# Attention and hard-swish MLP on one core: a planner that counts three modes of TensorE, finer constants, keys chosen anew

## The chip, the cores and the metric

The kernel runs on one core of a Trainium2 chip. The metric is the device time of one execution in microseconds (us). Three runs of the kernel before gave 583.2, 583.35 and 584.42 us; the median is 583.35 us.

## The reference

Causal attention over 4 batches and 12 heads (448 positions, head size 64), whose output becomes the 1792 x 768 input of a two-layer MLP with a hard-swish between the layers, all in float32.

```python
scores = scale * np.matmul(q, k.transpose(0, 1, 3, 2))
scores = np.where(mask, -1000000000.0, scores)       # causal
attn = np.exp(scores - max); attn = attn / (attn.sum + 1e-09)
x = (attn @ v) as 1792 x 768
h = x @ w_in                                          # 768 x 2048
g = h * np.clip(h + 3.0, 0.0, 6.0) / 6.0
out = g @ w_out                                       # 2048 x 768
```

## The kernel before, in words

The attention is cut into 24 units: a unit is one batch and one pair of heads. The MLP is cut by batch: batches 0 and 1 are computed alone (`first_layer`, `early_products`, `middle`), batches 2 and 3 together at the end with a Strassen-like scheme (`last_x`, `last_first`, `last_second`).

A unit is this chain. Scores: 8 row blocks (two heads e, four blocks i of 112 queries), in two operations, blocks 3 and 2 together and blocks 1 and 0 together (`products`, line 490). The two heads stand in the upper and the lower 64 rows of the array, so their matmuls run beside each other. Units 0 to 5 take float32 operands in one pass; the others split them in a high and a low part and take three matmuls each. Then VectorE adds the mask and takes the row minimum (line 505), ScalarE takes the exponential and its sum (line 512), VectorE the reciprocals (lines 522 and 523), and GpSimd, ScalarE or VectorE scale the rows (lines 533 and 531). TensorE turns the 20 blocks of 112 x 112 in six groups (line 553), ScalarE or VectorE copy each group from its PSUM bank (lines 361 and 364), and TensorE multiplies by v (line 566); there the two heads stand in two halves of 64 columns. The result is split into two parts again and is one of the MLP's operands.

Every product of the MLP is three matmuls of a 128 x 128 weight tile with 448 columns, on lines 640, 641 and 642. So TensorE's instructions are of three shapes: the whole array (lines 640 to 642, and the turns on line 553), two halves of rows (scores, line 490), two halves of columns (line 566).

The weights are made once from two 32-bit words each on VectorE (`words`, lines 603, 605 and 608), kept in DRAM and loaded again for later batches. ScalarE rounds them to a high part (line 361), VectorE or GpSimd subtract it for the low part (line 373).

The order of all this is not written by hand. `Flow` is a planner that runs while the program is built. Every operation has a key, made from a table of due times (`T_...`, `UNIT`, `LOADS`, `WORDS`, `K_...`), an expected duration, the engines that may take it, and what it reads and writes. At each step an engine takes the ready operation with the lowest key for which there is a buffer. Several engines may take the copies and the scalings; a lag says how much later one of them may. TensorE has one rule more: if the operation is of another mode than the last, the planner looks further for one of the same mode with a key at most `KEEP[mode]` later, and if it takes the other, it adds `SWITCH / 2` to the time. Before, there are two modes: `tiled` is true for scores and for the product with v, and false for all else, so going from one of these two to the other costs the planner nothing. Between 20 and 36 us of its own time the planner also writes in matmuls without use (`fill`, line 1072) where it expects TensorE to wait. At the start, `WARM` matmuls on a constant run before the first loads have landed (line 1092).

Of the kernel before, what the change touches and what calls it, by code (L numbers as in the profile page):

```python
# [19 lines left out]
C = 112  # L20
# [10 lines left out]

T_FIRST = -113
T_PACE = 4
T_EARLY = 8
T_EACH = 11
T_LATE = 74
T_DENSE = 7.25
T_LOAD = -8
T_W = 10
T_WLOAD = 9  # L40
T_XA = 166
T_X = 175
T_LAST = 182
T_PAIR = 10.5
T_SECOND = T_LAST + 8 * T_PAIR
T_SECOND_GROUP = 72
T_MID = 120
T_BACK = 40
T_WORDS = 77
M_LOAD = 20  # L50
E_WORDS = 6.5
K_SCORES = 0
K_TURN = 6.5
K_TURNS = 0.6
K_PRODUCT = 14
K_GATE = 5
KEEP_FULL = 0
KEEP_TILED = 6.5
N_RAW = 6
DEPTH = 3  # L60
A_FIRST = 4
D_FIRST = 0.4
T_V = 11
FINE = 3
W_FROM = 3
W_BEHIND = 4
UNIT = [-80, -17, 5, 2.5, 0.5, -1, -2, -1.5, 5.5, 0.5, -6.5, -3, -3.5, -8, -2.5, -4.5, -1, -1.5, -6, -4.5, -2.5, 1, -4, 3]
LOADS = [-70, -38, -8, 10, 0, -10, 12, -14, -22, -4, -20, -14, 10, 4, -12, 2, -8, -12, -2, -28, -10, -4, 4, -6]
K_KEEP = -4
K_G = 4  # L70
GATE_FROM = 1
WORDS = [1, 8, -6, 4, -3, 7, -5, 0, -4, 3, -6, 0, 6, -2, 7, -4, 2, 4, 2, 3, -2, 2, -8, -4, 8, 3, -7, 5]
T_ISSUE = 0.36
NORM_LAG = 1.5
A_LAG = 0

# [7 lines left out]
    qk="d qk", op="d op", wf="d wf", sf="d sf", x="d x", pt="d pt", pr3="d pr3", pr20="d pr20", xq="d xq", xc="d xc", gt="d gt", gm="d gm", so="d so",  # L84
    ps="b s most ps", tp="b s most", av="b s", mo="b mo", c="b c",
)
MOST = dict(qk=3, op=4, wf=4, sf=6, x=8, pt=6, pr3=4, pr20=5, xq=6, xc=21, gt=12, gm=9, so=3, s=8, most=8, ps=8, mo=2, c=8)

# [22 lines left out]
class Flow:  # L111
# [5 lines left out]
    BEGIN, LATENCY = 0.8, 0.12  # L117
    SWITCH = 0.4
    TAIL = dict(PE=.1, D=.085, A=.105, P=.04, SP=0)

    KEEP = KEEP_FULL, KEEP_TILED
    QUEUE, WARM = 8, 4
    DMA_PACKET, DMA_RATE, DMA_LANES, DMA_LATENCY = 0.008, 23e3, 16, 2.1
# [8 lines left out]

    def op(self, key, ways, parts, r=(), tiled=False, nbytes=0):

        w = [x for _, _, ws in parts for x in ws]
        bufs = {x[0] for x in list(r) + w if isinstance(x[0], Buf)}
        o = Op((key, len(self.ops)), ways, parts, bufs, nbytes)
        o.tiled = tiled
        for b in bufs:
            b.refs += 1  # L140
        before = {}
        for x in list(r) + w:
            if x in self.wrote:
                a, i = self.wrote[x]
                before[a] = max(before.get(a, 0), i)
        for x in w:
            for a in self.readers.pop(x, ()):
                before[a] = len(a.parts) - 1
        for x in r:
            self.readers.setdefault(x, []).append(o)  # L150
        for i, (_, _, ws) in enumerate(parts):
            for x in ws:
                self.wrote[x] = o, i
        before.pop(o, None)
        for a, i in before.items():
            a.then.append((o, i))
        o.waits = len(before)
        self.ops.append(o)
        return o

    def run(self):
# [3 lines left out]
        busy = dict.fromkeys(lists, self.BEGIN)  # L165
        self.dma, self.mode, self.port, tick = 0.0, False, 0.0, 0
        left = len(self.ops)
# [17 lines left out]
        while events:  # L185
            now = events[0][0]
            while events and events[0][0] <= now + 1e-9:
                _, _, what, x = heappop(events)
# [17 lines left out]
            for e, cand in lists.items():  # L206
# [4 lines left out]
                for _, o in cand:  # L211
# [9 lines left out]
                    for b in o.bufs:  # L221
                        if not b.held and b.kind in ORDERED:
                            x = turns[ORDERED[b.kind]]
# [41 lines left out]
    def start(self, o, e, now, need, out, busy, post):  # L265
# [5 lines left out]
        if e == "PE" and o.tiled != self.mode:  # L271
            t += self.SWITCH / 2
            self.mode = o.tiled
# [9 lines left out]
        if e == "SP":  # L283
            self.landed.append(o.ends[-1])
            t = max([t, *self.landed[-self.QUEUE:-self.QUEUE + 1]])
# [16 lines left out]
def tile_causal_attention_hardswish_moe(ctx: ExitStack, tc: tile.TileContext, q, k, v, w_in, w_out, out):  # L302
    nc = tc.nc
# [25 lines left out]
    def ap(b):  # L329
        if b.tile is None:  # L330
            b.tile = pools[b.tag].tile(b.shape, b.dt, tag=f"{b.tag}{b.slot}", name=b.tag, bufs=1)
        return b.tile
# [11 lines left out]

    def pe(key, parts, r, tiled=False):
        flow.op(key, {"PE": (1, 0)}, [(d, lambda e, g=g: g(), w) for d, g, w in parts], r, tiled)
# [35 lines left out]
    warm = const.tile([64, C], F32, tag="warm", name="warm")  # L382
# [37 lines left out]
    def unit(b, p):  # L420
        at = NPAIR * b + p
        raw32 = at < N_RAW
# [68 lines left out]

        cost, more = (1.667e-3, .06) if raw32 else (1.25e-3, .08)
        for a, two in enumerate(((1, 0), (3, 2)) if at == 0 else ((3, 2), (1, 0))):
# [3 lines left out]
                [(cost * C * (i + 1) + more, lambda i=i: products(i), [(ps[e, i][0], i) for e in range(2)] + [("turn",)]) for i in two],  # L497
                (halves_[0] if at == a == 0 else reads) + [("unit", at - (2 if b else DEPTH))], True,
            )
# [42 lines left out]
        for e in range(2):  # L542
            for js, ph in zip(GROUPS, pairs):
# [10 lines left out]

                pe(key, [(.096 * len(blocks) + .03, turn, [(tp, 0)])], [pk[e, i] for i in sorted({i for i, _ in blocks})])
                move(
# [13 lines left out]

        pe(t + K_PRODUCT, [(10 * C * 1.667e-3, times_v, [(av, 0), (av, 1), ("unit", at)])], deps, True)
        if b < 2:
# [518 lines left out]
    for _ in range(Flow.WARM):  # L1091
        nc.tensor.matmul(ap(b)[:C, :C], warm, warm, start=True, stop=True)

# [48 lines left out]
```

## Time and profile before

| | |
|---|---|
| runs, us | 583.2, 583.35, 584.42 |
| profiled execution, us | 583.93 |
| its span, first to last instruction, us | 582.2 |
| PE busy, us | 573.8 |
| DVE, ACT, POOL busy, us | 486.7, 405.7, 233.4 |
| TensorE matmul records | 3496 |

The span is 1.73 us shorter than the profiled execution; that much lies around it. The profiled execution is 0.58 us longer than the median of the runs. A matmul's busy time in the trace is longer than the distance to the next one's start, since matmuls overlap in the array: to see what a matmul costs, one subtracts the start of one row from the start of a later one. Consecutive instructions of one group are merged into one row, with their number behind an x. A float32 matmul that is not rounded stands in the trace as two records.

### The profile page before, as it was taken

Reading aid. Unit: us, or ns where it says so; the run is one execution under the profiler, and the core shown is the slowest. Engines: PE = TensorE matmul, PEld = TensorE weight load, DVE = VectorE, ACT = ScalarE, POOL = GpSimd, SP = SyncE. Lnnn points to the kernel's source line nnn. Section 1 sums busy time; section 2 is a strip of 40 time slices with the busy share of each in tenths; the row PEclk is TensorE's granted clock in tenths of the full one; section 3 lists DMA queues with packets and bytes.
Section 4 is the critical chain, followed back from the end, with each engine's and each line's share of the span. In section 5 each row is a group of like instructions: output and inputs, shape, how many; then the busy total and the mean of one; then the engine's idle time right before and its main releaser. Section 6 shows DMA issues by size and latency. Waiting matters only on the chain.

```text
span 582.2 us, 10686 instructions
## 1 busy us (share of the span) xinstructions
PE 573.8 (99%) x3496; PEld 502.5 (86%) x3496; DVE 486.7 (84%) x1093; ACT 405.7 (70%) x973; POOL 233.4 (40%) x226
## 2 busy tenths in 40 slices
PE   8999999999999999999999999999999999999997
PEld 5667988988888788888988989899999999999996
DVE  5899999899689787999998668999888799985652
ACT  6997885888757666899988968576555586454530
POOL 2678889874447344776274212034000042100000
PEclk9999999999999999999999999999999999999999
DMA  8958999967579898999832254441211424443411
GB/s 235 334 184 278 315 319 362 395 230 233 179 267 303 258 385 267 329 381 304 301 114 76 94 165 145 160 128 56 82 55 55 128 64 135 133 133 111 138 64 48
DMA packets 61352, 115.59 MB, mean 199 GB/s; under 512 B 6512, under 2 KB 36592, under 8 KB 61296
## 3 DMA queue, kind: packets, MB, share of 16 engines
q1 hardware_dynamic: 60576, 114.34, 59.5%
q10 hardware_dynamic: 720, 0.57, 0.3%
q8 instruction: 27, 0.44, 0.3%
q14 instruction: 29, 0.24, 0.1%
HBM read 83.39 MB, written 31.49 MB: 197 GB/s over the span
## 4 chain that ended last, share of the span: by engine, by line
PE 88%; DMA 5%; DVE 3%; ACT 2%; issue 1%; SPq 0%; DVEq 0%; ACTq 0%
PE b L640 24%; PE b L641 23%; PE b L642 23%; PE b L566 7%; PE b L553 6%; PE b L490 5%; DMA gl<-in_v_dram 2%; DMA wd<-in_w_in_dram 1%; DMA wd<-in_w_out_dram 1%; ACT d L512 1%; DVE b L603 1%; DVE d L608 1%; DVE b L505 1%; DVE b L605 1%; ACT gl L512 0%
## 5 line engine op out<-in xcount | busy, mean ns | idle before, releaser
L640 PE MATMUL b<-d,wh 128*128 128x448 f32 x624 | 231.4, 371 | 0.7 <-ACT d L512 0.7
L641 PE MATMUL b<-d,wh 128*128 128x448 f32 x624 | 226.3, 363 | 0.0
L642 PE MATMUL b<-d,wl 128*128 128x448 f32 x624 | 225.7, 362 | 0.0
L640 PEld LDWEIGHTS b<-d,wh 128*128 128x128 f32 x624 | 117.2, 188 | 10.6 <-ACT d L512 1.2
L642 PEld LDWEIGHTS b<-d,wl 128*128 128x128 f32 x624 | 116.9, 187 | 9.0 <-POOL wl L373 0.4
L641 PEld LDWEIGHTS b<-d,wh 128*128 128x128 f32 x624 | 117.2, 188 | 6.3
L361 ACT CAST wh<-wd 128x768 fp32r<-128x768 f32 x88 | 73.6, 836 | 70.1 <-PE b L641 61.5
L373 DVE TENSOR_TENSOR wl<-wd,wh 128x768 fp32r<-128x768 f32 x74 | 79.7, 1077 | 26.0 <-ACT wh L361 25.0
L505 DVE CUSTOM_DVE_ANT_0 b<-b,mask 112x224 f32<-112x224 f32 (+1 forms) x192 | 80.2, 479 | 19.6 <-PE b L490 17.2
L512 ACT ACTIVATE d<-b,prow 112x448 f32<-112x448 f32 (+2 forms) x144 | 72.2, 517 | 15.5 <-DVE prow L505 13.1
L373 POOL TENSOR_TENSOR d<-d 128x896 fp32r<-128x896 f32 (+3 forms) x28 | 43.2, 1548 | 36.3 <-DVE d L373 23.4
L553 PE MATMUL b<-ident,d 112*112 112x112 f32 x384 | 55.9, 261 | 1.2 <-ACT d L512 0.8
L373 POOL TENSOR_TENSOR wl<-d,wh 128x768 fp32r<-128x768 f32 (+1 forms) x28 | 46.1, 1649 | 23.9 <-ACT wh L361 14.9
L361 ACT COPY d<-b 112x336 f32<-112x336 f32 (+1 forms) x104 | 43.7, 494 | 7.5 <-PE b L553 6.9
L553 PEld LDWEIGHTS b<-ident,d 112*112 112x112 f32 x384 | 42.7, 133 | 5.6 <-POOL gl L533 1.0
L533 POOL TENSOR_SCALAR d<-d,prow 112x112 f32<-112x112 f32 (+2 forms) x59 | 29.4, 509 | 31.7 <-DVE prow L523 25.4
L566 PE MATMUL b<-d,vr 112*64 112x224 f32 (+3 forms) x288 | 37.5, 405 | 0.0
L531 ACT ACTIVATE d<-d,prow 112x336 f32<-112x336 f32 (+2 forms) x66 | 33.8, 548 | 4.2 <-DVE prow L523 4.2
L603 DVE TENSOR_SCALAR b<-wd 128x384 int32<-128x384 int32 (+1 forms) x56 | 32.9, 613 | 3.0 <-DMA wd<-in_w_out_dram 2.5
L490 PE MATMUL b<-d 64*112 64x448 f32 (+3 forms) x432 | 35.0, 305 | 0.0
L490 PEld LDWEIGHTS b<-d 64*112 64x112 f32 x432 | 30.2, 172 | 5.5 <-issue 1.2
L566 PEld LDWEIGHTS b<-d,vr 112*64 112x64 f32 x288 | 19.1, 136 | 18.4 <-issue 10.7
(111 smaller groups left out, 934.3 us busy)
## 6 DMA issues: line engine op xcount, KB each, us to landing
wd<-in_w_in_dram SPq DMA_DIRECT2D x32, 384.0 KB, 6.0
wd<-in_w_out_dram SPq DMA_DIRECT2D x24, 512.0 KB, 6.6
wd<-kept_w SPq DMA_DIRECT2D x32, 384.0 KB, 4.7
wd<-kept_s SPq DMA_DIRECT2D x32, 384.0 KB, 3.0
kept_w<-d SPq DMA_DIRECT2D x16, 384.0 KB, 6.2
kept_w<-d SPq DMA_DIRECT2D x24, 256.0 KB, 5.4
kept_s<-d SPq DMA_DIRECT2D x24, 256.0 KB, 3.8
wd<-kept_w SPq DMA_DIRECT2D x48, 128.0 KB, 2.2
```

The costliest lines, as they stand in the source:

```text
L361: nc.scalar.copy(o(), i()) if scale is None else nc.scalar.mul(o(), i(), scale)
L373: (nc.gpsimd if e == "P" else nc.vector).tensor_tensor(o(), a(), b(), op)
L490: nc.tensor.matmul(score(e, i), qx[m, c], kx[m, :w], start=n == 0, stop=n == len(terms) - 1)
L505: lambda _, e=e, i=i, w=w: nc.vector.tensor_tensor_reduce(score(e, i), score(e, i), mask[:, S - w:], -0.125, 3.0e38, ALU.add, ALU.min, ap( ...
L512: lambda _, e=e, i=i: nc.scalar.activation(row_of(pr, e, i), score(e, i), ACTF.Exp, bias=ap(st)[:, e, i:i + 1], scale=-1.0, accum_out=ap(s ...
L531: nc.scalar.mul(x, x, ap(st)[:, e, 4 + i:5 + i])
L553: nc.tensor.transpose(ap(tp)[:C, C * n:C * n + C], row_of(pr, e, i)[:, C * j:C * j + C], ident)
L566: nc.tensor.matmul(ap(av)[64 * e:64 * e + 64, S - w:S], va()[:, j, e, :], ap(ph)[:, e, o:o + w], start=(j == 0), stop=(j == NC_ - 1),)
L603: nc.vector.tensor_scalar(ti, high, 3, 0x3FFFFFFF, ALU.logical_shift_left, ALU.bitwise_and)
L640: nc.tensor.matmul(ps, ap(wh)[:, a], xh, start=start, stop=False, skip_group_check=more)
L641: nc.tensor.matmul(ps, ap(wh)[:, a], xl, start=False, stop=False, skip_group_check=more)
L642: nc.tensor.matmul(ps, ap(wl)[:, a], xh, start=False, stop=stop, skip_group_check=more)
```

## The change

The planner's modes become three: 0 for the whole array, 1 for scores, 2 for the product with v. A change between any two costs 0.1 us of planned time, where a change between tiled and not tiled cost 0.2 us before. `KEEP` has an entry for each mode: from the whole array another mode may be left aside for an operation due at most 0.5 later (0 before), in either of the other two for 6 (6.5 before). The expected time of a score block goes from 0.08 to 0.09 us beside its columns, that of a product with v gets 0.07 us more, and that of a group of turns 0.03 us less. At the start 11 matmuls of 56 columns take the place of 4 of 112. Due times, keys, lags and numbers of buffers are new throughout.

```diff
-T_FIRST = -113
-T_PACE = 4
+T_FIRST = -94
+T_PACE = 6.5
...
-T_LOAD = -8
+T_LOAD = -20
-T_WLOAD = 9
+T_WLOAD = 14
...
-M_LOAD = 20
+M_LOAD = 11
...
-KEEP_FULL = 0
-KEEP_TILED = 6.5
+KEEP_FULL = 0.5
+KEEP_TILED = 6
...
-A_FIRST = 4
-D_FIRST = 0.4
+A_FIRST = 3.2
+D_FIRST = 0
...
-UNIT = [-80, -17, 5, 2.5, ...]
+UNIT = [-72, -19, 5, 4.5, ...]
...
-MOST = dict(qk=3, op=4, wf=4, sf=6, x=8, pt=6, pr3=4, pr20=5, xq=6, xc=21, gt=12, gm=9, so=3, s=8, most=8, ps=8, mo=2, c=8)
+MOST = dict(qk=3, op=4, wf=3, sf=8, x=8, pt=9, pr3=5, pr20=5, xq=6, xc=21, gt=12, gm=8, so=3, s=8, most=8, ps=8, mo=4, c=8)
...
-    SWITCH = 0.4
+    SWITCH = 0.1
...
-    KEEP = KEEP_FULL, KEEP_TILED
-    QUEUE, WARM = 8, 4
+    KEEP = KEEP_FULL, KEEP_TILED, KEEP_TILED
+    QUEUE, WARM = 8, 11
...
-            t += self.SWITCH / 2
+            t += self.SWITCH
...
-        cost, more = (1.667e-3, .06) if raw32 else (1.25e-3, .08)
+        cost, more = (1.667e-3, .06) if raw32 else (1.25e-3, .09)
...
-                (halves_[0] if at == a == 0 else reads) + [("unit", at - (2 if b else DEPTH))], True,
+                (halves_[0] if at == a == 0 else reads) + [("unit", at - (2 if b else DEPTH))], 1,
...
-                pe(key, [(.096 * len(blocks) + .03, turn, [(tp, 0)])], [pk[e, i] for i in sorted({i for i, _ in blocks})])
+                pe(key, [(.096 * len(blocks), turn, [(tp, 0)])], [pk[e, i] for i in sorted({i for i, _ in blocks})])
...
-        pe(t + K_PRODUCT, [(10 * C * 1.667e-3, times_v, [(av, 0), (av, 1), ("unit", at)])], deps, True)
+        pe(t + K_PRODUCT, [(10 * C * 1.667e-3 + .07, times_v, [(av, 0), (av, 1), ("unit", at)])], deps, 2)
...
-        nc.tensor.matmul(ap(b)[:C, :C], warm, warm, start=True, stop=True)
+        nc.tensor.matmul(ap(b)[:C, :C // 2], warm, warm[:, :C // 2], start=True, stop=True)
```

What this does to the order is seen at three places.

TensorE, among the first units, behind the turns of unit 1 (L553): L1072 are the matmuls without use, L490 the scores of unit 3. A minus is a row of before alone.

```order
 L553 MATMUL b<-ident,gl 112x112
 L553 MATMUL b<-ident,d 112x112 x5
-L1072 MATMUL b<-identr 112x112 x4
 L490 MATMUL b<-gh 112x448 x2
 L490 MATMUL b<-gh 112x336 x2
```

The four matmuls without use are gone here, and likewise the four at a second place, behind the turns of unit 2.

TensorE, in the first layer of batch 0, around one product with v (L566) and one unit's scores (L490), before:

```order
L642 MATMUL b<-d,wl 128x448
L566 MATMUL b<-d,vr 64x448 x2
L566 MATMUL b<-d,vr 64x336 x2
L566 MATMUL b<-d,vr 64x224 x2
L566 MATMUL b<-d,vr 64x112 x2
L490 MATMUL b<-d 112x448 x6
L490 MATMUL b<-d 112x336 x6
L490 MATMUL b<-d 112x224 x6
L490 MATMUL b<-d 112x112 x6
L640 MATMUL b<-d,wh 128x448
```

The same place now:

```order
L566 MATMUL b<-d,vr 64x448 x2
L566 MATMUL b<-d,vr 64x336 x2
L566 MATMUL b<-d,vr 64x224 x2
L566 MATMUL b<-d,vr 64x112 x2
L640 MATMUL b<-d,wh 128x448
L641 MATMUL b<-d,wh 128x448
L642 MATMUL b<-d,wl 128x448
L490 MATMUL b<-d 112x448 x6
L490 MATMUL b<-d 112x336 x6
L490 MATMUL b<-d 112x224 x6
L490 MATMUL b<-d 112x112 x6
L640 MATMUL b<-d,wh 128x448
```

Products of the MLP now stand between the product with v and the scores, so TensorE goes through three shapes with one change more. Counted over the whole program, without the matmuls without use, the changes between the three shapes go from 69 to 83; 15 of them lay among the first six units and 16 do now. The trips from the MLP's products to turns, which have the same shape, go from 51 to 31 (3 and 4 of them among the first six units). Counted as the planner did before, whole array against any half, the changes go from 47 to 75.

ScalarE, around the exponentials of unit 3 (L512), before; L361 are copies of turned blocks (112 rows) and of the products with v (128 rows):

```order
L361 COPY d<-b 112x448
L361 COPY d<-b 112x336 x2
L512 ACTIVATE d,prow<-b,prow 112x448 x2
L512 ACTIVATE d,prow<-b,prow 112x336
L361 CAST d<-b 128x448
L361 COPY r<-b 128x448
L512 ACTIVATE d,prow<-b,prow 112x336
L361 COPY d<-b 112x448
L361 COPY d<-b 112x336 x2
L361 COPY d<-b 112x448
L512 ACTIVATE gl,prow<-b,prow 112x224 x2
```

The same place now:

```order
L361 CAST d<-b 128x448
L361 COPY r<-b 128x448
L512 ACTIVATE d,prow<-b,prow 112x448 x2
L512 ACTIVATE d,prow<-b,prow 112x336 x2
L512 ACTIVATE gl,prow<-b,prow 112x224 x2
L512 ACTIVATE d,prow<-b,prow 112x112 x2
L512 ACTIVATE d,prow<-b,prow 112x448 x2
L512 ACTIVATE d,prow<-b,prow 112x336 x2
L512 ACTIVATE gl,prow<-b,prow 112x224 x2
L512 ACTIVATE d,prow<-b,prow 112x112 x2
```

The copies of unit 2's turned blocks have left ScalarE's queue here; they stand on VectorE's now. Ahead of the last exponential of unit 5 there were 14 copies of turned blocks on ScalarE and are 7.

## Rows read from the trace of the kernel before

**Rows 1.** The page's first part: busy us, share of the span, instructions.
```profile
span 582.2 us, 10686 instructions
PE 573.8 (99%) x3496; PEld 502.5 (86%) x3496; DVE 486.7 (84%) x1093; ACT 405.7 (70%) x973; POOL 233.4 (40%) x226
```

**Rows 2.** Waits of PE from 60 us to the end: us, times, longest.
```profile
PE b L640 <- ACT d L512: 0.7, 1, 0.7
```

**Rows 3.** Timeline of PE near 100 us: start, us, instruction.
```profile
98.40 0.37 PE L642 MATMUL b<-d,wl 128*128 128x448 f32 x1
98.70 2.11 PE L566 MATMUL b<-d,vr 112*64 112x448 f32 x16
100.74 1.89 PE L490 MATMUL b<-d 64*112 64x448 f32 x24
...
102.87 0.37 PE L641 MATMUL b<-d,wh 128*128 128x448 f32 x1
103.07 0.37 PE L642 MATMUL b<-d,wl 128*128 128x448 f32 x1
```

**Rows 4.** Timeline of PE around scores alone, near 212 us.
```profile
211.02 0.36 PE L642 MATMUL b<-d,wl 128*128 128x448 f32 x1
...
213.66 0.37 PE L642 MATMUL b<-d,wl 128*128 128x448 f32 x1
```

**Rows 5.** Timeline of PE around a product with v alone, near 365 us.
```profile
363.83 0.37 PE L642 MATMUL b<-d,wl 128*128 128x448 f32 x1
...
366.68 0.36 PE L642 MATMUL b<-d,wl 128*128 128x448 f32 x1
```

**Rows 6.** Timeline of PE around ten turned blocks, near 120 us.
```profile
119.32 0.37 PE L642 MATMUL b<-d,wl 128*128 128x448 f32 x1
...
119.63 0.74 PE L553 MATMUL b<-ident,d 112*112 112x112 f32 x6
120.20 0.26 PE L553 MATMUL b<-ident,pr 112*112 112x112 f32 x1
...
120.91 0.37 PE L642 MATMUL b<-d,wl 128*128 128x448 f32 x1
```

**Rows 7.** Timeline of PE among the first units.
```profile
21.98 0.60 PE L1072 MATMUL b<-identr 112*112 112x112 f32 x4
22.64 1.57 PE L490 MATMUL b<-gh 64*112 64x448 f32 x8
...
47.69 3.99 PE L566 MATMUL b<-d,gl 112*64 112x448 f32 x32 [0.17 <-DVE d L608]
```

**Rows 8.** Busy us of each engine (instructions) from 16 to 52 us, granted clock, DMA.
```profile
16.00:52.00 36.00, 35.25 (x281) 24.29 (x283) 33.06 (x112) 32.19 (x102) 27.15 (x43) 1.00 0.77 254
```

**Rows 9.** Groups by line: busy us, mean ns of one, idle before.
```profile
L361 ACT COPY d<-b 112x336 f32<-112x336 f32 (+1 forms) x104 | 43.7, 494 | 7.5 <-PE b L553 6.9
```

**Rows 10.** Timeline of DVE, three of its waits.
```profile
10.27 0.63 DVE L505 CUSTOM_DVE_ANT_0 b<-b,mask 112x448 f32<-112x448 f32 x1 [1.34 <-PE b L490]
...
21.10 0.17 DVE L522 TENSOR_SCALAR b<-prow 112x8 f32<-112x8 f32 x1 [1.60 <-ACT d L512]
...
209.65 0.69 DVE L603 TENSOR_SCALAR b<-wd 128x512 int32<-128x512 int32 x1 [1.74 <-DMA wd<-in_w_out_dram]
```

**Rows 11.** Timeline of POOL before unit 3's scalings.
```profile
32.56 1.84 POOL L373 TENSOR_TENSOR wl<-d,wh 128x768 fp32r<-128x768 f32 x1 [3.71 <-ACT wh L361]
```

**Rows 12.** Groups of POOL with 896 elements: busy, mean ns.
```profile
L368 POOL TENSOR_SCALAR d<-d 128x896 fp32r<-128x896 f32 x9 | 9.3, 1030 | 14.3 <-issue 6.3 <-PE b L490 6.2 <-DVE d L533 1.8
```

**Rows 13.** Timeline of PE at the start.
```profile
1.08 1.83 PE L1092 MATMUL b<-warm 64*112 64x112 f32 x8 [1.08 <-DVE warm L385]
...
3.58 4.08 PE L490 MATMUL b<-gh 64*112 64x224 f32 x16 [0.67 <-DMA gh<-in_k_dram]
```

**Rows 14.** Scores (line 490) of unit 1 and of unit 2: PE, PEld busy, clock, DMA.
```profile
8.42:12.15 3.73, 3.73 (x16) 2.41 (x18) 1.00 1.07 294
12.21:14.12 1.91, 1.91 (x19) 1.33 (x17) 1.00 1.06 253
```

More of the change, by code (lines that the diff above doesn't have):

```diff
@@ L37 @@
 T_DENSE = 7.25
-T_LOAD = -8
+T_LOAD = -20
 T_W = 10
-T_WLOAD = 9
-T_XA = 166
-T_X = 175
-T_LAST = 182
+T_WLOAD = 14
+T_XA = 165
+T_X = 172
+T_LAST = 180
 T_PAIR = 10.5
-T_SECOND = T_LAST + 8 * T_PAIR
+T_SECOND = 266
 T_SECOND_GROUP = 72
@@ L49 @@
 T_WORDS = 77
-M_LOAD = 20
+M_LOAD = 11
 E_WORDS = 6.5
 K_SCORES = 0
[L53 to L56, printed above, removed]
-KEEP_FULL = 0
-KEEP_TILED = 6.5
+K_TURN = 7
+K_TURNS = 0.5
+K_PRODUCT = 13
+K_GATE = 4
+KEEP_FULL = 0.5
+KEEP_TILED = 6
 N_RAW = 6
 DEPTH = 3
-A_FIRST = 4
-D_FIRST = 0.4
-T_V = 11
+A_FIRST = 3.2
+D_FIRST = 0
+T_V = 6
 FINE = 3
@@ L66 @@
 W_BEHIND = 4
[L67 to L70, printed above, removed]
+UNIT = [-72, -19, 5, 4.5, 0, -3.5, -8, 1, 4, 3.5, -6, -4, -4.5, -7.5, -8, -2.5, 1, -4.5, -2.5, -8, -6, 0.5, -5, 3]
+LOADS = [-58, -36, -8, 6, 4, -18, 2, -16, -28, -20, 12, 2, -2, -6, -6, -30, -28, -28, -14, 10, -2, -4, 8, -4]
+K_KEEP = -6
+K_G = 5
 GATE_FROM = 1
-WORDS = [1, 8, -6, 4, -3, 7, -5, 0, -4, 3, -6, 0, 6, -2, 7, -4, 2, 4, 2, 3, -2, 2, -8, -4, 8, 3, -7, 5]
+WORDS = [-2, -4, -6, -1, 3, 2, -8, -1, 6, -5, 2, 5, 5, 8, 5, -5, 3, 0, -5, 4, -3, -5, 5, -3, 5, 3, 8, 3]
 T_ISSUE = 0.36
-NORM_LAG = 1.5
-A_LAG = 0
+NORM_LAG = 0.5
+A_LAG = 0.8
 BUFS = dict(
@@ L131, in __init__, with op @@
         self.ops, self.wrote, self.readers, self.landed = [], {}, {}, []
-    def op(self, key, ways, parts, r=(), tiled=False, nbytes=0):
+    def op(self, key, ways, parts, r=(), tiled=0, nbytes=0):
         w = [x for _, _, ws in parts for x in ws]
         bufs = {x[0] for x in list(r) + w if isinstance(x[0], Buf)}
-        o = Op((key, len(self.ops)), ways, parts, bufs, nbytes)
+        o = Op((round(key, 5), len(self.ops)), ways, parts, bufs, nbytes)
         o.tiled = tiled
@@ L165, in run @@
         busy = dict.fromkeys(lists, self.BEGIN)
-        self.dma, self.mode, self.port, tick = 0.0, False, 0.0, 0
+        self.dma, self.mode, self.port, tick = 0.0, 0, 0.0, 0
         left = len(self.ops)
@@ L343, in one, with pe @@
             o.port = set()
-    def pe(key, parts, r, tiled=False):
+    def pe(key, parts, r, tiled=0):
         flow.op(key, {"PE": (1, 0)}, [(d, lambda e, g=g: g(), w) for d, g, w in parts], r, tiled)
```

## The prediction

> **What bounds the kernel now.** I read the page's first part, then PE's waits, then the timeline of PE, and at last what the other engines do where PE waits. PE is busy for 573.8 of 582.2 us and no other engine for more than 486.7 [rows 1]. That share alone proves little, since a matmul's busy time overlaps the next one's; so the waits were read. From 60 us to the end PE waits once, 0.7 us, for a bank that ScalarE frees [rows 2]. Among the first units, from 16 to 52 us, it is busy for 35.25 of 36.00 us, and there DVE (33.06) and ACT (32.19) are nearly full as well [rows 8]. So the time is made of three things: the start up to the first scores, the matmuls themselves, and what TensorE loses when it changes its shape. The matmuls of the reference are the same before and after (2088 of the MLP, 480 of scores, 192 with v, 480 turns). What is left to differ is the changes of shape, the waits, and the start.
>
> **Changes of shape.** What does one cost? Three pieces of the timeline answer it together. Each runs from one MLP matmul to the third one after the strange work, so each holds three MLP distances of 0.20 us (102.87 to 103.07). A product with v and a unit's scores in one trip: 98.40 to 103.07, 4.67 us [rows 3]. Scores alone: 211.02 to 213.66, 2.64 us [rows 4]. A product alone: 363.83 to 366.68, 2.85 us [rows 5]. The two alone make 5.49 us, the two together 4.67; the difference of 0.82 holds three MLP distances, 0.60, and the rest, 0.22 us, is the one change more that two trips have (four against three). The second place shown of the order is just this split. Each of the four starts is rounded to 0.01 us and the places differ a little, so I allow 0.18 to 0.26.
>
> The order has 14 changes more, 13 of them after the first six units: 13 x 0.22 = 2.9 us. Against this there are fewer trips to turns. One with ten turned blocks takes 119.32 to 120.91, 1.59 us, less three MLP distances 0.99 us; six turns take 119.63 to 120.20, 0.57 us, so ten take 0.95, and the trip costs 0.04 us [rows 6]. After the first units there are 48 such trips before and 27 now: 21 x 0.04 = 0.8 us go. Sum: +2.1 us, all on the path that sets the end, because PE waits nowhere there. Bounds 1.5 to 2.6 us.
>
> The Trainium skill, page "TensorEngine Tiling (Array Packing)", section Tiling Modes, says that a change of tiling mode, though not of the tile, drains the engine. By that rule rows against columns is a change like any other, and the count is 14; the 0.22 us agree. If only leaving and entering the whole array cost anything, as the planner held before, the split place would have two changes more and not one, the count would be 28 (75 - 47), and at half the price each, 0.11 us, it would come to 3.1 us in place of 2.9, which makes 583.9 us of the forecast below.
>
> **The first six units.** Two groups of matmuls without use go. One of them stands from 21.98 to 22.64 us, 0.66 us [rows 7]; the second repeats it, together 1.3 us. The scores behind each come after turns, a change of 0.2 us that stays, so 0.9 us at most come free, if the scores' operands and banks are ready then. The plain waits in this stretch are 36.00 - 35.25 = 0.75 us [rows 8]. Both together, 1.7 us, are what this stretch can give back by the rows.
>
> Will it? These waits are for the engines behind the scores. The scores' chain goes through ScalarE's exponentials, and DVE's longest wait in this stretch, 1.60 us at 21.10, is for them [rows 10]. Ahead of unit 5's last exponential ScalarE now has 7 copies fewer, and 3 scalings more, priced like a copy: 4 x 0.49 = 2.0 us less in its queue [rows 9]. The copies land on VectorE, which has fewer steps of the weights' making ahead (6 in place of 12 before unit 3's scores are done), so its queue is about as long as before. GpSimd gets the split of unit 6 ahead of unit 3's scalings; a cast of 896 elements is 1.03 us and the subtraction behind it more [rows 12], but GpSimd stood idle for 3.71 us there [rows 11]. That idle time is the cover, and if unit 6's loads are late, the cover is gone and unit 3's scalings wait behind it in GpSimd's queue, and the turns behind them. I take the whole 1.7 us, since PE had next to nothing else to wait for, and for the other end +0.6 us, a shift of a wait with nothing given back and one of about the size of the second filler put in its place. The product with v of unit 4 starts at 47.69, held by VectorE [rows 7]; it is the place where the gain has to be seen.
>
> **The start.** The 11 narrow matmuls have 11 x 56 = 616 columns in place of 4 x 112 = 448. The old ones take 1.83 us from 1.08 [rows 13]; by columns the new ones take 2.5 us and end at 3.6 us, just when the first loads have landed, at 3.58. So they cost nothing to 0.1 us, hidden by the loads; if the loads came earlier, they would be in the way by what is left of them. TensorE runs its first scores at the lower of its levels (1.2 GHz): unit 1's 16 records take 3.73 us, unit 2's 1.91, and the step lies at 12.15 us; the column of the granted clock reads 1.00 in both stretches, so the step is read from the pace [rows 14]. I take no change here. Bounds: an earlier step gives back at most DVE's wait for unit 1's scores, 1.34 us [rows 10], and nothing is lost.
>
> **Later waits and loads.** PE's 0.7 us [rows 2] comes from weights that VectorE makes late: VectorE waits 1.74 us for words from DRAM [rows 10], and the scores' masks, the exponential and the bank stand behind. These late words are held by a step of the MLP, which the change leaves, so the larger T_WLOAD doesn't bring them forward; I leave the 0.7 us in. The shorter lead of the loads in `middle` (M_LOAD 20, now 11) costs nothing while its cover holds, the other operations of TensorE between issue and use. Bounds for all later waits: -0.7 us, and +1.0, a bit more than one new wait like the present one.
>
> **Sum.** 583.93 (the profiled execution) + 2.1 - 1.7 + 0 + 0 = 584.33 us. It was 0.58 us above the median of its runs, so 583.75 against 583.35: I say 583.7 us. About 0.2%, 1.2 us, is what a measurement can tell here, so this is no change, with 582.2 and 584.5 as its limits.
>
> **Rivals.** *The waits of the first units only move* (slower). Mechanism: VectorE holds the product of unit 4 at 47.69 by its own queue, which does not get shorter, so PE comes there earlier and waits there longer. For it: DVE is busy 33.06 of 36.00 us, more than ACT. Against it: 1.60 us of what it waited was for ScalarE. Time: 583.35 + 2.1 = 585.4 us. It decides as soon as that product starts at 47.5 us or later. Chance 0.24.
>
> *All that can be freed is freed* (faster): the first units give 1.7 us, the late wait's 0.7 goes too, and the changes cost 0.18, which makes 1.5: 583.35 + 1.5 - 1.7 - 0.7 = 582.4; with the start's clock on top, at half its 1.34 us, 581.8 us. For it: the late wait hangs on one order of VectorE's queue, and all orders are new. Against it: it needs three things at once, though gaps that the modelled ends hide in the first units would help. Chance 0.24, mostly below 582.2.
>
> *The clock alone*: the longer stretch of early matmuls brings TensorE's step to 2.4 GHz forward, ahead of unit 1's scores, while the rest is as forecast: 583.7 less half of 1.34 is 583.0 us. For it: the gap between the early matmuls and the first scores, 0.67 us [rows 13], closes. Against it: the gap before unit 1's scores stays, since they wait for loads. Chance 0.10. The Trainium skill, page "TensorE: Matmul & The Clock Gate", Part 1, holds the lower clock to be the default that sustained activity releases; this rival goes by that rule, and the one step in the trace neither bears it out nor speaks against it.
>
> My forecast has the remaining 0.42.
>
> **How the numbers follow.** Faster by over 0.2%: 0.21 of the rival that frees all, 0.05 of the forecast's own spread, 0.03 of the clock: 0.29. Slower: 0.22 of the rival of moved waits, and 0.07 of the forecast, where a new later wait comes in: 0.29. Same: 0.42. The forecast's own range is 582.2 to 584.9. The range from 581.5 to 585.6 takes in both outer rivals and leaves out at the top new waits beyond one, at the bottom a clock that gives all of 1.34 us.
>
> **What would show it.** Right: a split trip of product and scores costs 0.2 us more than the joint one also in the new trace; no matmul of line 1072 left; the product of unit 4 starts near 46 us; one or two waits of PE after 60 us, together under 1.5 us. Wrong: the product of unit 4 at 47.5 us or later, waits of PE in `middle`, a step of the clock ahead of unit 1's scores, or a change of shape that costs 0.1 us as the planner says.

## The result, and the profile after

The changed kernel takes 588.29 us (median of 4 runs, 587.87 to 589.04), the kernel before, on the same chip, 583.28 us (4 runs, 582.43 to 584.42): a ratio of 1.0082, with an interval of 1.0063 to 1.0102. So it is 5.0 us slower, where 583.7 was forecast, and outside the range. The profiled execution took 589.04 us, 5.11 more than that of before.

The first part of the page after, in the columns of [rows 1]:

```profile
span 587.3 us, 10737 instructions
PE 577.9 (98%) x3502; PEld 504.5 (86%) x3502; DVE 490.6 (84%) x1101; ACT 395.5 (67%) x939; POOL 260.8 (44%) x252
```

PE is busy 4.1 us longer, and the span grew by 5.1: there is more to do and more to wait for. The waits of PE from 60 us to the end, where [rows 2] had one of 0.7 us:

```profile
PE b L640 <- DVE d L608: 1.4, 1, 1.4
PE b L553 <- DVE pr L533: 0.5, 1, 0.5
```

The timeline of PE around a place where a product with v and a unit's scores are now two trips, answering to [rows 3 to 5]:

```profile
102.19 0.37 PE L642 MATMUL b<-d,wl 128*128 128x448 f32 x1
102.48 2.11 PE L566 MATMUL b<-d,vr 112*64 112x448 f32 x16
104.52 0.47 PE L640 MATMUL b<-d,wh 128*128 128x448 f32 x1
...
105.03 0.36 PE L642 MATMUL b<-d,wl 128*128 128x448 f32 x1
...
105.63 0.36 PE L642 MATMUL b<-d,wl 128*128 128x448 f32 x1
105.92 1.90 PE L490 MATMUL b<-d 64*112 64x448 f32 x24
107.75 0.48 PE L640 MATMUL b<-d,wh 128*128 128x448 f32 x1
...
108.27 0.36 PE L642 MATMUL b<-d,wl 128*128 128x448 f32 x1
```

Each trip is read as in the prediction, from one MLP matmul to the third one behind. The product costs 105.03 - 102.19 = 2.84 us, the scores 108.27 - 105.63 = 2.64 us; together 5.48, less 0.60 for three more MLP distances, against 4.67 in one trip [rows 3]: 0.21 us for the change more.

The same rows say what the step from the product to the scores costs. The product takes 2.04 us from its first start to the next one, whether scores come next (98.70 to 100.74) or the MLP (102.48 to 104.52). The scores take 1.82 us behind the product (from 100.74 to the row below, of before) and 1.83 behind the MLP (105.92 to 107.75). So this step is not free: it costs what leaving the product for the MLP and entering the scores from the MLP cost together.

```profile
102.56 0.47 PE L640 MATMUL b<-d,wh 128*128 128x448 f32 x1
```

The start, PE's timeline, answering to [rows 13], with the first turn and the product of unit 4:

```profile
1.08 4.17 PE L1092 MATMUL b<-warm 64*112 64x56 f32 x21 [1.08 <-DVE warm L385]
4.87 0.71 PE L490 MATMUL b<-gh 64*112 64x224 f32 x1
...
5.23 9.88 PE L490 MATMUL b<-gh 64*112 64x224 f32 x47
15.75 0.28 PE L553 MATMUL b<-ident,d 112*112 112x112 f32 x1 [0.63 <-ACT d L512]
...
49.50 3.99 PE L566 MATMUL b<-d,gl 112*64 112x448 f32 x32
```

The 11 early matmuls are 22 records, 21 in the first row and the last between the first two of the scores, until 5.23 us: one every 0.19 us, as in [rows 13] (1.83 us for 8), though each has half the columns. The first scores come 1.3 us later than in [rows 13], and PE waits for no load at all: the operands were there. Where does this reach? VectorE's masks show it, answering to [rows 10]; the first row is the first mask of before, the second the same mask after, the third the sums of unit 0 after:

```profile
5.20 0.40 DVE L505 CUSTOM_DVE_ANT_0 b<-b,mask 112x224 f32<-112x224 f32 x1 [3.44 <-PE b L490]
```

```profile
6.81 0.40 DVE L505 CUSTOM_DVE_ANT_0 b<-b,mask 112x224 f32<-112x224 f32 x1 [5.04 <-PE b L490]
...
12.00 0.17 DVE L522 TENSOR_SCALAR b<-prow 112x8 f32<-112x8 f32 x1 [0.30 <-ACT d L512]
```

The wait of 1.34 us for unit 1's scores [rows 10] is gone: TensorE's records keep the pace of 2.4 GHz from 7.6 us on, ahead of these scores, where the step lay at 12.15 before [rows 14]. So VectorE runs through from 7.87 on but for 0.30 us at 12.00. All of the 1.34 us that the prediction set as a bound came back, but the first mask comes 1.6 us later than before, which is more.

PE's waits from 0 to 60 us (us in total, times, longest), and the stretch from 16 to 52 us, answering to [rows 8]:

```profile
PE b L553 <- ACT d L512: 0.9, 2, 0.6
PE b L553 <- DVE d L364: 0.4, 2, 0.2
PE b L490 <- ACT d L512: 0.4, 1, 0.4
PE b L553 <- ACT d L361: 0.3, 1, 0.3
```

```profile
16.00:52.00 36.00, 34.36 (x264) 23.38 (x264) 33.39 (x115) 30.77 (x98) 27.06 (x43) 1.00 0.66 226
```

Last, the chain of waits of the changed kernel near 180 us: start, us, what.

```profile
171.74 4.23 DMA kept_w<-d
...
178.74 7.09 DMA d<-kept_w
...
187.98 0.70 DVE d L608
188.72 0.47 PE b L640
```

Between 165 and 190 us the chain of before consists of PE's instructions alone. Here it goes through two transfers: a part of the weights goes to DRAM, comes back 7.09 us after its issue, and VectorE then makes the next words in three steps of 0.7 us, for which PE waits at 188.72.

Where the 4.89 us between the two last matmuls' ends went, summed over the distances between the starts of all matmul records: the product of unit 5 ends at 53.42 in place of 51.62 us, 1.80 later, but by then three MLP matmuls (0.6) more are done and one change (0.2) less, so 1.4 is lost. Behind that the changes of shape cost 13.03 us (67 of them) in place of 10.16 (54), the trips to turns 0.80 in place of 1.30: +2.4, and 2.2 net of the change saved early. Late waits, the hidden ones with them, take 3.25 in place of 1.68 us: +1.6. These make 5.2; 0.3 too much lie in rounded distances. The trace of before has 71 changes, and not the 69 counted ahead of the prediction: the two from the matmuls without use to scores were left out there. So the changes grow by 12 over the whole program, 13 more behind the first units and one less in them (17 before, 16 now); whole array against any half go from 49 to 75, 26 more and not 28. The last 1000 MLP matmuls take 199.80 us in both.

### The profile page after: what moved, and what is told of

The parts are those of the page before. It is cut to its first block, busy times and chain, and to the rows that moved or that the text cites. A ratio compares the mean times of both kernels' runs of the same rounds, so it can differ in the third digit from the quotient of the medians.

```text
span 587.3 us, 10737 instructions
## 1 busy us (share of the span) xinstructions
PE 577.9 (98%) x3502; PEld 504.5 (86%) x3502; DVE 490.6 (84%) x1101; ACT 395.5 (67%) x939; POOL 260.8 (44%) x252
## 4 chain that ended last, share of the span: by engine, by line
PE 86%; DVE 6%; DMA 3%; ACT 3%; issue 1%; SPq 0%; DVEq 0%
PE b L640 23%; PE b L642 23%; PE b L641 22%; PE b L566 6%; PE b L553 6%; PE b L490 5%; DMA wd<-in_w_out_dram 1%; ACT d L512 1%; DVE d L364 1%; DMA d<-kept_w 1%; DVE b L505 1%; ACT gl L512 1%; DVE b L605 1%; DVE b L603 1%; DMA kept_w<-d 1%
## 5 line engine op out<-in xcount | busy, mean ns | idle before, releaser
L361 ACT CAST wh<-wd 128x768 fp32r<-128x768 f32 x88 | 73.5, 836 | 81.2 <-PE b L641 74.0
L373 DVE TENSOR_TENSOR wl<-wd,wh 128x768 fp32r<-128x768 f32 x67 | 70.1, 1046 | 22.6 <-ACT wh L361 21.4
L512 ACT ACTIVATE d<-b,prow 112x448 f32<-112x448 f32 (+2 forms) x144 | 72.4, 516 | 16.7 <-DVE prow L505 12.5
L553 PE MATMUL b<-ident,d 112*112 112x112 f32 x384 | 53.2, 260 | 1.3 <-ACT d L512 0.6
L373 POOL TENSOR_TENSOR wl<-d,wh 128x768 fp32r<-128x768 f32 (+1 forms) x27 | 43.7, 1623 | 23.8 <-ACT wh L361 19.0
L373 POOL TENSOR_TENSOR wl<-wd,wh 128x768 fp32r<-128x768 f32 x21 | 38.8, 1850 | 23.3 <-ACT wh L361 10.2
L373 POOL TENSOR_TENSOR d<-d 128x512 f32<-128x512 f32 (+2 forms) x24 | 38.9, 1628 | 23.0 <-DMA wd<-in_w_out_dram 7.5
L553 PEld LDWEIGHTS b<-ident,d 112*112 112x112 f32 x384 | 41.7, 133 | 4.5 <-POOL gl L533 0.8
L373 POOL TENSOR_TENSOR wd<-wd 128x384 f32<-128x384 f32 x17 | 17.1, 1019 | 59.1 <-DVE wl L373 21.8
L361 ACT COPY d<-b 112x336 f32<-112x336 f32 (+1 forms) x92 | 38.0, 483 | 6.6 <-PE b L553 3.7
L566 PE MATMUL b<-d,vr 112*64 112x224 f32 (+3 forms) x288 | 37.1, 404 | 0.1
L490 PEld LDWEIGHTS b<-d 64*112 64x112 f32 x432 | 30.0, 172 | 7.5 <-issue 2.4
L373 DVE TENSOR_TENSOR d<-d 128x448 fp32r<-128x448 f32 (+3 forms) x42 | 31.7, 770 | 4.7 <-DMA d<-kept_w 1.9
```

The lines of the kernel that those rows point to most:

```text
L361: nc.scalar.copy(o(), i()) if scale is None else nc.scalar.mul(o(), i(), scale)
L373: (nc.gpsimd if e == "P" else nc.vector).tensor_tensor(o(), a(), b(), op)
L490: nc.tensor.matmul(score(e, i), qx[m, c], kx[m, :w], start=n == 0, stop=n == len(terms) - 1)
L512: lambda _, e=e, i=i: nc.scalar.activation(row_of(pr, e, i), score(e, i), ACTF.Exp, bias=ap(st)[:, e, i:i + 1], scale=-1.0, accum_out=ap(s ...
L553: nc.tensor.transpose(ap(tp)[:C, C * n:C * n + C], row_of(pr, e, i)[:, C * j:C * j + C], ident)
L566: nc.tensor.matmul(ap(av)[64 * e:64 * e + 64, S - w:S], va()[:, j, e, :], ap(ph)[:, e, o:o + w], start=(j == 0), stop=(j == NC_ - 1),)
```

## The experiments

The kernel before stood at 583.1 to 583.7 us in each comparison; "old" and "new" mean the plan of before and of the change. The quoted text behind each edit is what was expected before its run.

**The start, undone in the new plan (new_old_start), and done alone in the old (old_new_start).**

```diff
-    QUEUE, WARM = 8, 11
+    QUEUE, WARM = 8, 4
...
-        nc.tensor.matmul(ap(b)[:C, :C // 2], warm, warm[:, :C // 2], start=True, stop=True)
+        nc.tensor.matmul(ap(b)[:C, :C], warm, warm, start=True, stop=True)
```

> The changed kernel, only the start as before: 4 matmuls of 112 columns, no other instruction moved. Theory: the 22 records of the 11 narrow ones end at 5.23 us and hold the first scores 1.65 us, but they bring the clock's step from 12.15 to 7.64 us, so the first turns come only 0.56 us later; undone, the first scores are back at 3.58, the step at about 12 us, and the time falls by 0.6 us to 587.7. Rival: the whole 1.65 us reaches the end, 586.6. Rival: the earlier step is worth more than the delay, so the time rises.

> The kernel before, only the start as changed (11 narrow matmuls). Theory: first scores at 5.2 us, clock's step near 7.6 us, first turns 0.5 us later, time 583.9. Rival: the 1.65 us reach the end, 584.9.

Undone: 586.5 us, ratio to before 1.0048 (1.0033 to 1.0063), 1.8 us less than the change. Alone: 585.28 us, 1.003 (1.0013 to 1.0046), 1.8 us more by the medians of that comparison and 1.75 by the ratio. Both lie nearer to the rivals (586.6 and 584.9) than to the theory (587.7 and 583.9): in the new plan the start costs about 1.8 us, against 0 in the forecast. In the old plan the size is the same, but proves less: two edits below that delay nothing at the start cost the old plan 1.2 and 1.6 us as well, by the ratios. What is left, 2.8 us (1.0048), belongs to the plan.

**More or narrower early matmuls.** old_six has six of 112 columns in the old plan (WARM = 6), new_eight eight of them in the new plan, new_narrow_weights keeps the 11 but gives them weights of 56 columns too:

```diff
-        nc.tensor.matmul(ap(b)[:C, :C // 2], warm, warm[:, :C // 2], start=True, stop=True)
+        nc.tensor.matmul(ap(b)[:C // 2, :C // 2], warm[:, :C // 2], warm[:, :C // 2], start=True, stop=True)
```

> The kernel before with 6 early matmuls of 112 columns in place of 4: 12 records of 0.187 us, which end near 3.4 us, before the first loads at 3.58. Theory: nothing is delayed; if the gap before the first scores is what kept the clock low, the step comes near 7.6 us and the first turns up to 1 us earlier, 582.3 to 583.0; if not, it stays at 12 us and the time at 583.3.

> The changed kernel, the 11 early matmuls with weights of 56 columns too. Theory: a record's pace was set by its weights of 112 columns (0.187 us), so now it is 0.093 us, the 22 records end at 3.1 us, the first scores are at 3.58 again, and the time falls by at least 0.6 us to 587.7, by up to 1.5 us if the clock's step stays near 7.6 us. Rival: a record costs 0.187 us whatever its shape: nothing changes, 588.3.

> The new plan with 8 early matmuls of 112 columns: 16 records of about 0.187 us from 1.08 us end near 4.07, some 0.5 us behind the landing of the loads at 3.58, and the first scores start near 4.1 in place of 3.36 (four early matmuls) and 4.87 (eleven). If the delay of the first scores reaches the end whole, the time is 586.5 + 0.7 = 587.2 us, about halfway to 588.3. Rival: only the clock or the count of columns matters; then 8 x 112 = 896 columns, more than the 616 of the changed kernel, cost at least as much as it: 588.3 or more.

Measured: old_six 584.13 us, 1.0009 (0.999 to 1.0027); new_narrow_weights 586.78, 1.0056 (1.0035 to 1.0077); new_eight 586.7, 1.0048 (1.003 to 1.0067). PE's timeline at the start of new_narrow_weights and of new_eight:

```profile
1.08 2.30 PE L1092 MATMUL b<-warm 64*56 64x56 f32 x22 [1.08 <-DVE warm L385]
3.36 4.08 PE L490 MATMUL b<-gh 64*112 64x224 f32 x16
...
14.28 0.28 PE L553 MATMUL b<-ident,d 112*112 112x112 f32 x1 [0.81 <-ACT d L512]
```

```profile
1.09 3.14 PE L1092 MATMUL b<-warm 64*112 64x112 f32 x15 [1.09 <-DVE warm L385]
...
4.21 2.83 PE L490 MATMUL b<-gh 64*112 64x224 f32 x15
7.98 6.01 PE L490 MATMUL b<-gh 64*112 64x448 f32 x32 [0.94 <-DMA gh<-in_k_dram]
```

With narrow weights the same 22 records take half the time, and the first scores are not late: here the weights' columns set the pace, not those of the other operand (56 in both). The Trainium skill, page "TensorE: Matmul & The Clock Gate", Part 2, section Step-by-step, says that loading weights takes a time that goes by their columns; the distance of 0.19 against 0.09 us per record agrees. new_eight shows that the count of columns isn't what costs (896, more than the changed kernel's 616, and 1.6 us less), and its time is that of four early matmuls within 0.2 us, though its first scores are 0.5 to 0.8 us late. Two things in its trace take this delay away. Its records go over to the pace of 2.4 GHz while unit 0's scores still run: these take 3.20 us, from 3.84 (their first record, between the last early ones) to 7.04, and end ahead of the 7.44 of new_old_start (3.36 + 4.08). And TensorE then waits 0.94 us for unit 1's keys. In the changed kernel the scores of unit 0 end too late for that wait. So how much of a delay reaches the end without an earlier step is not shown by new_eight.

None of the three takes less time than its plan with four early matmuls, so a step of the clock that comes early is worth nothing at the end. Here one reading of the prediction was at fault. Twelve of the profiles have the old start, and the first turn lies between 13.93 and 15.19 us, the mean at 14.44, because unit 1's keys land and the step of the clock falls at another place in each execution: unit 1's scores start between 7.74 and 8.52 us, and the step lies at 12.15 us before, but already among unit 0's scores in rules_alone (3.65 us in place of 4.08). PE's first turn before, and in a kernel with the same start (old_without_fillers, below):

```profile
15.19 0.28 PE L553 MATMUL b<-ident,d 112*112 112x112 f32 x1 [0.81 <-ACT d L512]
```

```profile
13.93 0.28 PE L553 MATMUL b<-ident,d 112*112 112x112 f32 x1 [0.63 <-ACT d L512]
```

The profile of before is the latest of the twelve. VectorE's wait for unit 1's scores, 1.34 us there [rows 10], goes from 0 to 1.34 among them, is absent in four and is 0.59 on the mean. With the new start the first turn lay at 15.75 us in both profiles, so it costs 1.31 us at this place against the mean, not 0.56 as the two profiles alone say. The Trainium skill, page "TensorE: Matmul & The Clock Gate", Part 1, section What's actually happening, warns that the number of matmuls ahead of the step varies from run to run; the twelve agree.

**The plan, by halves.** rules_alone has the planner's rules and costs of the change with the old keys and the old start, keys_alone the new keys with the old rules and start. Of the rules:

```diff
-    SWITCH = 0.4
+    SWITCH = 0.1
-    KEEP = KEEP_FULL, KEEP_TILED
+    KEEP = KEEP_FULL, KEEP_TILED, KEEP_TILED
...
-            t += self.SWITCH / 2
+            t += self.SWITCH
```

> The planner's new rules (three modes, 0.1 us a change, the finer expected times) with all keys, tables and the start of before. By the order, the changes of shape after the first six units are 68 (54 before), the trips to turns 38 (48). Theory (each change costs 0.2 us, paid in full): 14 x 0.21 - 10 x 0.04 = +2.5 us, 586.0, give or take a late wait of 1 us. Rival (the keys make the loss): 583.5, no change.

> The new keys and tables with the planner's rules and the start of before. By the order, 62 changes after the first six units (54 before) and 18 among them (15), trips to turns 32 (48). Theory: 8 x 0.21 + 3 x 0.2 - 16 x 0.04 = +1.6 us, 585.1, give or take a late wait. Rival (the rules make the loss): 583.5. Rival (the keys bring waits of their own): over 586.

601.02 us, 1.0317 (1.0284 to 1.0349), and 596.24 us, 1.0209 (1.0166 to 1.0252): far above what was expected, both. They have 68 and 62 changes of shape behind the first units, about the new plan's 67, so the changes explain 3 of 18 and 2 of 13 us. The rest is mostly waiting, and in part the clock: three of the four executions of each show a mean granted clock of 0.991 to 0.994, and the fourth of keys_alone, at 1.000, took 592.14 us. PE's waits from 60 us on, first the largest of nine lines in rules_alone, then the largest of three in keys_alone:

```profile
PE b L553 <- ACT d L512: 2.1, 2, 1.1
```

```profile
PE b L553 <- DVE d L608: 4.4, 3, 2.7
```

So keys and rules belong together: each half, with the other as it was, costs more than the whole, and neither says what its part of the change is worth.

**The groups without use, taken from the old plan (old_without_fillers).**

```diff
-                out.append((self.idle + self.FILL * i, len(out), "PE", lambda _, m=self.mode: self.filler(b, m), set()))
+                pass
```

> The kernel before without the 8 matmuls without use on line 1072, every other instruction in its place. Forecast's view: TensorE had nothing to wait for there, so 0.9 us come free, 582.6. Rival: TensorE waits for the scores' operands and banks there anyway, the waits show in their place, 583.3.

584.5 us, 1.0028 (1.001 to 1.0046). The 1.3 us of these matmuls give nothing back: from the first turn to the end of unit 5's product PE takes 36.44 us (13.93 to 50.37), and 36.43 before (15.19 to 51.62). The time even rises, by 0.6 to 2.7 us, which neither side expected; why is open.

**The price of a change, by itself.** In the products of the last layer, where PE waits for nothing, matmuls of 56 columns are put in at 84 places: in tail_joint two with halves of rows (S) and two with halves of columns (P) behind each other, in tail_mixed alternating, in tail_split the two kinds at different places. Each ran once, under the profiler.

```diff
+                            extra(ap(banks[m]), wh, 'SSPP' if c % 2 else '')
...
+                            extra(ap(banks[m]), wh, 'SPSP' if c % 2 else '')
...
+                            extra(ap(banks[m]), wh, 'PP' if c % 2 else 'SS')
```

> The kernel before with four small extra matmuls at 84 places among the MLP's last products (behind every second triple of last_second): two of the scores' shape, then two of the product's shape with v (S S P P), 3 changes of shape a place. They are no part of the computation and write columns that nothing reads. It is the base for the next two, with the same extra matmuls.

> The same 84 places with the order S P S P: 5 changes a place, all two more of them between rows and columns. Theory (0.17 to 0.19 us each): 84 x 0.36 = 30 us above the joint one. Planner before (nothing between these two): 0 us. Planner now (0.1 us): 17 us.

> The same extra matmuls with S S behind the even triples and P P behind the odd ones: 4 changes a place. Theory (0.22 us for an extra trip): 84 x 0.21 = 18 us above the joint one. Planner now: 8 us. If only changes between the whole array and a half cost, two more of them a place: 34 us or more.

The first lines of the three pages, in this order:

```profile
span 649.2 us, 11694 instructions
```

```profile
span 678.9 us, 11694 instructions
```

```profile
span 664.4 us, 11694 instructions
```

Mixed against joint has two changes more at each of 84 places, rows against columns: 29.7 us / 168 = 0.177 us for each. But this is an upper bound, for the order takes something else away as well. In joint the two of kind P stand in two halves of columns and run beside each other; in mixed they are apart. PE's timeline at one place of tail_joint, then of tail_mixed (L1008 is kind P):

```profile
500.07 0.33 PE L1008 MATMUL b<-ident 112*64 112x56 f32 x4
500.33 0.47 PE L640 MATMUL b<-d,wh 128*128 128x448 f32 x1
```

```profile
503.49 0.32 PE L1008 MATMUL b<-ident 112*64 112x56 f32 x2
503.74 0.29 PE L1006 MATMUL b<-identr,wh 64*128 64x56 f32 x1
```

Both take 0.26 us together in joint, and each takes 0.25 us in mixed (the second from 503.96 to 504.21). That is most of the 0.354 us (29.7 / 84) that a place costs more, so tail_mixed doesn't say what rows against columns costs by itself. Split against joint has no such flaw and one more trip: 15.2 / 84 = 0.18 us, near the forecast's price and not the 0.1 of the planner now. It doesn't tell the forecast from the count of whole array against any half at 0.11 us a change, which makes 18 us too. That the step from rows to columns is not free is shown by the kernel's own rows, 2.04 us for the product in either place.

**Where the late waits come from.** The trace puts PE's late waits down to VectorE's words (L608). old_light_late_words and new_light_late_words (this with the old start) leave out two of the three steps with which VectorE makes the late words of w_out:

```diff
-            if step == 0:
+            if kind == "sf":
+                if step == 2:
+                    nc.vector.tensor_scalar(ap(wf)[:, o:o + m].bitcast(I32), low, 29, 0x3FFFFFFF, ALU.logical_shift_right, ALU.bitwise_and)
+            elif step == 0:
```

> The kernel before, where the second half of w_out is made in one step on VectorE in place of three and without a PSUM bank; it leaves out two of three steps, so these weights are not the reference's. Theory: PE's late wait of 0.9 us near 215 us goes, 582.6. Rival: the wait moves elsewhere, 583.5.

> The changed kernel with the start of before and the same lighter making of the second half of w_out (two of three steps left out). Theory: its late waits near 187 to 217 us (1.7 to 3.2 us) come from VectorE's late words and their banks and go: 584.5 to 584.9, and 2.0 to 2.4 us stay between this kernel and the one before with the same edit, the changes of shape. Rival: the waits come from loads and stay, 586.5.

584.24 us, 1.0021 (1.0009 to 1.0032), and 585.36 us, 1.0037 (1.0027 to 1.0047). With less work for VectorE the old plan got no faster but 1.2 us slower, and the new one at most 0.6 us faster than new_old_start, with intervals that overlap. Between the two 1.1 us stay, where 2.0 to 2.4 were expected. In the old plan a wait came in that it did not have; PE's timeline of old_light_late_words:

```profile
188.83 0.31 PE L553 MATMUL b<-ident,pr 112*112 112x112 f32 x1 [1.51 <-ACT d L512]
```

In the new plan the wait for VectorE's words did go. PE's waits from 60 us on in new_old_start, then in new_light_late_words:

```profile
PE b L640 <- DVE d L608: 1.5, 1, 1.5
```

```profile
PE b L553 <- DVE gh L678: 0.6, 1, 0.6
```

So VectorE's steps are a part of what the late wait of the new plan hangs on, though little of it is won at the end, and in the old plan another wait takes the place. The other part is its operands: the DMA engines are busy for 0.95 of the time from 180 to 220 us before, and 0.99 after (span, PE, PEld, DVE, ACT, POOL, clock, DMA share, GB/s; before, then after):

```profile
180.00:220.00 40.00, 39.30 (x263) 33.69 (x262) 33.62 (x84) 28.11 (x76) 22.27 (x23) 1.00 0.95 328
```

```profile
180.00:220.00 40.00, 37.83 (x253) 32.07 (x250) 33.42 (x82) 25.93 (x69) 20.77 (x18) 1.00 0.99 330
```

old_more_loads and new_more_loads (the old start in both) put one more copy of 128 KB, from DRAM to DRAM, behind each of the twelve late loads of w_out:

```diff
+                first(out=out, in_=in_)
+                first(out=more, in_=in_[:, :1])
```

> The old plan with the old start; each of the 12 late loads of in_w_out is followed on SP's queue by one more copy of 128 KB from DRAM to DRAM, 12 x 0.26 MB of traffic beside the work and nothing on an engine. If TensorE's late waits (185 to 217 us) hang on the transfers, this plan, which has them short (about 1 us), gets more of them: 2 us or more in the trace of waits after 60 us, 585.5 us. Rival: they hang on VectorE's queue, which this leaves as it is: no wait more, 583.3 us, within 1 us.

> The same 12 copies in the new plan with the four old early matmuls (586.5 us without the copies). Transfers: its late waits of 1.75 us grow by 2 us or more, 588.5 us. VectorE's queue: the same within 1 us, 586.5.

585.48 us, 1.0027 (1.0016 to 1.0039), and 590.03 us, 1.0104 (1.0083 to 1.0125), against 1.0048 without the copies: 3.3 us, more than the theory of the transfers said. The old plan's time is near what it said, but PE's waits after 60 us grew by 1.0 us (0.7 to 1.7) in place of 2, and 1.6 us is what the old plan lost without its fillers too. PE's late wait in new_more_loads, and what comes behind it (its line numbers are 7 or 8 higher):

```profile
188.41 0.47 PE L648 MATMUL b<-d,wh 128*128 128x448 f32 x1 [2.27 <-DVE d L616]
...
191.00 0.57 PE L649 MATMUL b<-d,wh 128*128 128x448 f32 x1
191.38 0.57 PE L650 MATMUL b<-d,wl 128*128 128x448 f32 x1
```

By the distance of the starts the wait is 2.50 us, and was 1.75 without the copies; behind the longer one two matmuls lie 0.38 us apart in place of 0.20, until the step back near 193 us. The copies go through the same queue and the same memory as the loads, so it is shown for the new plan that its late wait grows with the transfers ahead of VectorE's steps; whether by the queue of issues or by the rate of the engines is not told apart. For the old plan it is not shown.

No experiment gave a version that beats the kernel before; the nearest, old_six, is no different from it.

## Why the prediction was wrong

**Right: the price of a change.** Forecast 0.22 us each (0.18 to 0.26) and +2.1 us in all; measured 0.21 at one place, 0.22 on the mean of the thirteen (13.03 - 10.16 over 13), 0.18 in the tail (tail_split), and +2.4 with the turns behind the first units, +2.2 in all, since the order has 12 changes more and not 14. The turns gave back 0.5 in place of 0.8. As the price of a trip more the planner's 0.1 us is half of what was measured. That rows against columns is a change like any other, as the prediction had it, is borne out by the 2.04 us of the product in both places; tail_mixed gives only an upper bound for it, 0.177 us.

**Wrong: the start.** The step that failed is "by columns the new ones take 2.5 us and end at 3.6 us". The duration was scaled from [rows 13] by the columns of the moving operand, while the weights stayed 112 wide, and so did the time of a record. It comes to 22 x 0.19 = 4.2 us, to 5.2, well past the loads' landing at 3.58. "They cost nothing to 0.1 us, hidden by the loads" fell with it, and so did the bound "nothing is lost", which had no row behind it. It cost 1.3 us at the first turn and about 1.8 us at the end. The text even named the condition (they are in the way by what is left of them), without working out a price for it.

**The clock.** The rival's step did come ahead of most of unit 1's scores and did take away VectorE's 1.34 us. But this wait was that of one execution, the longest of twelve. The mean is 0.59, less than the half of 1.34 that the rival took, and even that did not arrive (old_six).

**Wrong: the first six units, -1.7.** The two groups without use are gone, and from 16 to 52 us PE is idle for 36.00 - 34.36 = 1.64 us in place of 0.75 [rows 8]: of the 1.3 us of these groups 0.9 is idle time now. From the first turn to the end of unit 5's product PE takes 37.64 us with the old start (14.85 to 52.49) and 36.43 before (15.19 to 51.62). Less 0.6 for three MLP matmuls more, and with 0.2 for one change less, that is 0.8 lost, where 1.7 was to be won. In the old plan old_without_fillers won nothing (36.44). "PE had next to nothing else to wait for" was the step that failed: removing work from an engine that stands beside two nearly full ones turned it into waits. The rival of moved waits was right in this, and its 585.4 us is near the time with the old start (1.0048 x 583.35 = 586.1); its sign, the product of unit 4 at 47.5 us or later, came true (49.50; 48.57 with the old start). Its mechanism was not quite: that product waits for nothing now, and the waits stand ahead of turns and scores, for ScalarE's exponentials and for banks that ScalarE or VectorE copy.

**Wrong: the later waits, 0.** Forecast -0.7 to +1.0; by the distances +1.6 in the changed kernel and +0.1 with the old start (1.75 against 1.68). The step that failed is that the shorter lead "costs nothing while its cover holds, the other operations of TensorE between issue and use". What it left out is the way of the words to TensorE: transfers, whose engines were at 0.95 of their time already, and VectorE's three steps behind them. No row of the transfers was read for the later stretch.

Sum by the runs: start +1.8 (in the traces 0.9 of it up to unit 5, the rest in late waits), changes and turns +2.2, first units +0.8, and 0.2 for late waits of the plan and what varies between executions: 5.0. What stays open: why a delay of 1.3 us at the first turn is 1.8 at the end, while earlier first turns (old_six 14.17 and new_narrow_weights 14.28 against the mean of 14.44) bring nothing. Late waits that start by another execution's timing are a possible cause, not shown.

## What to carry to other kernels

The early matmuls took as long with half the moving columns, as long as their weights kept 112: halving one operand is priced by a row with both shapes, and matmuls that fill a wait need to end before what is waited for lands. A wait read from one execution, above all one that hangs on the clock's step, is a sample: its price is the mean over executions. Where TensorE stood next to two nearly full engines, work taken from it came back as waiting. And an edit that is to isolate one cost must leave alone which matmuls run beside each other.

## What the runs showed of the hardware

The clock falls again in the middle of a kernel: in new_more_loads the distance of two MLP matmuls went from 0.20 to 0.38 us after a wait of 2.27 us and was 0.20 again from 193.72 on, and in keys_alone after waits of 2.66 and 1.87 us; behind the wait of 1.44 us at 188.72 in the changed kernel it stayed at 0.20. PE's timeline of keys_alone, where the distance is 0.37 behind the wait, and the stretch from 188 to 192 us of new_more_loads, whose granted clock is 0.69:

```profile
200.77 0.31 PE L553 MATMUL b<-ident,pr 112*112 112x112 f32 x1 [2.66 <-DVE d L608]
...
202.10 0.57 PE L642 MATMUL b<-d,wl 128*128 128x448 f32 x1
202.47 0.57 PE L640 MATMUL b<-d,wh 128*128 128x448 f32 x1
```

```profile
188.00:192.00 4.00, 3.59 (x14) 3.23 (x15) 3.20 (x14) 2.32 (x9) 4.00 (x3) 0.69 1.10 386
```

The lower pace is near that of half the clock, 1.2 GHz. A wait can thus cost more than its length: in new_more_loads six distances of 0.38 in place of 0.20 us add 1.1 us, about half of the wait itself. Five of its six executions show a mean granted clock of 0.994 to 0.997; the sixth, at 1.000, took 587.64 us, 2.4 less than the median.
